# Router rounds, gathers and weight scales of the later experts placed later in TensorE's queue

## The chip, the cores and the metric

One NeuronCore of one Trainium2 chip. The metric is the device time in microseconds (us) of one execution. Engines are named as in the profile: PE is TensorE's matmul side and PEld its weight loads, DVE is VectorE, ACT is ScalarE, POOL is GpSimd, SP is SyncE.

## What is computed

Three layers in a row: an attention with 32 memory slots, an expert layer whose router fills eight experts of 576 tokens each, and a dense gated layer.

```python
# attention, per batch (8) and head (8), sequence 576, head size 64, 32 slots
a = softmax(phi over the sequence);  k_m = a^T k;  v_m = a^T v
x = softmax(q k_m^T / 8) v_m                      # x: 4608 tokens x 512
# expert layer: 8 experts, capacity 4608 / 8 = 576 tokens
logits = x @ w_gate
for idx in argsort(-logits.flatten()):            # best (token, expert) pairs first
    tok, e = idx // 8, idx % 8
    if assigned[tok] >= 0 or counts[e] >= cap: continue
    assigned[tok] = e; counts[e] += 1
out[mask_e] = relu(x[mask_e] @ w1[e]) @ w2[e]     # 512 -> 1024 -> 512
# dense layer, all tokens
h = out @ w_in;  out = (h * clip(h + 3, 0, 6) / 6) @ w_out     # 512 -> 2048 -> 512
```

## The kernel before

The first part, up to about 250 us, is the attention (a software pipeline over 36 steps); it writes x to DRAM (`xd`) and keeps the router's logits in SBUF (`LG`). The second part does the experts two at a time. For each pair P of experts (2P and 2P+1) TensorE runs, in this order: `l1(2P)` (x times w1, tiles `p<-xt,w` of 128x288), `l2(2P)` (times w2, tiles `p<-h,w`), `l1(2P+1)`, `l2(2P+1)`, and `l34(P)`, the dense layer on the pair's 1152 tokens. `l34` is 48 steps; each step is 12 matmuls `p<-yt,wi` of 128x384 (times w_in) and, two steps behind, 9 matmuls `acc<-wo,h` of 128x512 (times w_out). All operands are split in a high and a low fp16 half, so that each product takes three matmuls. Between the two halves of a step ACT, DVE, ACT and POOL turn `p` into the two fp16 halves of `h`.

Experts are found one after the other. `route(k)` finds the expert that fills up next. In up to eight rounds it counts, for 15 thresholds at a time, how many free tokens prefer each expert above the threshold (nine matmuls `rtp<-Bo,C` on the comparison tile `C`, L794; four that add them up, L803; one that spreads the result to all partitions, L812). Then it counts once more (`ce`, L854), numbers the chosen tokens by a prefix sum (`tot`, L881 and L882), and turns the numbers into a list of token indices `ix` by 36 matmuls with one-hot tiles `OH` (L951, in six groups of six; each OH tile is a DVE instruction of 128x768, three buffers). The last expert's route has no rounds. `gathers` then fetches the tokens' rows of `xd` by five indirect DMAs on POOL's queue (`xg<-xd,ix`, two buffers from the third expert on, so that the next fetch follows a transposition), transposes them on TensorE (`xp<-ident,xg`, L623) and lets ACT and DVE write the two halves of `xt`. `weights` fetches the expert's w1 and w2 (`wst`, indirect DMAs on POOL's queue), finds their scale (squares on ACT, `ws` and `s_...m` on DVE, a maximum over the partitions by a TensorE transposition `amx`, L694) and splits them on ACT and DVE (`w<-wst,s`). `ysplit` does the same for the experts' outputs (`sy_...`). Routes 0 and 1 run before the first pair; routes 2P+2 and 2P+3 run inside `l34(P)`, from its step 16 on (`R_OK`).

All this is one instruction stream per engine, and the place of each instruction in it is set when the kernel is built. A clock (`CK.now`) adds up an estimated cost of every dense matmul in `mm`. The router, the gathers, the weights and the evictions are Python generators. After every dense matmul `run` resumes each generator whose time has come; a generator writes its instructions to the streams there and yields the clock time at which it wants to go on, mostly `V_.t + HOP`, the estimated end of DVE's work plus 0.25. So a small matmul that waits for DVE is put into TensorE's stream behind the dense matmuls that the clock thinks will cover DVE's work. TensorE executes its stream in that order.

```python
    def mm(o, l, r, start, stop, cost):
        nc.tensor.matmul(o, l, r, start=start, stop=stop)
        CK.now += cost
        run()
```

The places that the change touches: `all_max` (L688) and `pow2` (L700) for the scales, `route` (L737; its yields at L792, L852, L879 and L942), `weights` (the call of `pow2` at L1009), `gathers` (`fetch`, the time at which a gather counts as landed, L1075) and `ysplit` (L1353).

Of the kernel before, what the change touches and what calls it, by code (L numbers as in the profile page):

```python
# [20 lines left out]
def attn_moe_kernel(ctx: ExitStack, tc: tile.TileContext, q, k, v, phi, w_gate, w1, w2, w_in, w_out, out):  # L21
# [68 lines left out]
    with tc.tile_pool(name="ald", bufs=2) as ald, tc.tile_pool(name="aw", bufs=2) as aw, \  # L90
# [354 lines left out]
        for t in range(-LEAD - 4 - PRE, NTK + A1 + 2):  # L445
# [72 lines left out]
            if t in DT:  # L518
                tag, m = DT[t]
# [60 lines left out]
    V_ = Eng(nc.vector, 0.1, 0.00105)  # L580
    A_ = Eng(nc.scalar, 0.06, 0.00097)
    G_ = Eng(nc.gpsimd, 0.1, 0.0022)
    HOP = 0.25
    DQ = [0.0]

    def dma(cost, issue=None):
        DQ[0] = max(DQ[0], (CK.now if issue is None else issue) + 1.8) + cost
        return DQ[0] + 0.3
# [96 lines left out]
    half_c = rt.tile([128, 1], F32, name="half_c")  # L685
    nc.vector.memset(half_c, 0.5)

    def all_max(m, f):  # L688
        yield V_.t + HOP
        done = [False]  # L690
        while len(MMQ) >= 4 and not MMQ[0][0]:
            yield CK.now + 0.05
        p = mm_tile([128, 128], "amx", done)
        nc.tensor.matmul(p, m.bitcast(F32).to_broadcast([128, 128]), ident, start=True, stop=True)  # L694
        CK.now += 0.22
        yield CK.now + HOP
        V_.tensor_reduce(f, p, axis=AX.X, op=OP.max)
        done[0] = True

    def pow2(src, name, sq, lo, target):  # L700
        m = rt.tile([128, 1], I32, name=name + "m", tag="scm_", bufs=4)
        f = rt.tile([128, 1], F32, name=name + "f", tag="scf_", bufs=4)
        o = rt.tile([128, 2], F32, name=name)
        oi = o.bitcast(I32)
        if sq:
            V_.tensor_scalar(m, src.bitcast(I32), 24, 23, op0=OP.logical_shift_right, op1=OP.logical_shift_left)
            t = target + 127 + 63
        else:
            V_.tensor_scalar(m, src.bitcast(I32), 0x7F800000, None, op0=OP.bitwise_and)
            V_.tensor_scalar(m, m, float(lo << 23), None, op0=OP.max)  # L710
            t = target + 127 + 127
        yield from all_max(m, f)
        SR[0] = SR[0] or sq
        f = f.bitcast(I32)
        V_.tensor_scalar(oi[:, 0:1], f, -1.0, float(t << 23), op0=OP.mult, op1=OP.add)
        V_.tensor_scalar(oi[:, 1:2], f, float((254 - t) << 23), None, op0=OP.add)
        yield V_.t + HOP
        return o
# [16 lines left out]
            yield from route(k)  # L735

    def route(k):  # L737
        V = rt.tile([128, NT], F32, name="V")
        B1 = rt.tile([128, NT, E], F32, name="B1", tag="BC")
        bm = rt.tile([128, NT], F32, name="bm")  # L740
# [20 lines left out]
        else:  # L761
            TH = TH0
            for i in range(NST):
                C = rt.tile([128, NT, 15], BF16, name="C")
                p = ps.tile([128, 64], F32, name="rtp")
                if k == 0:
                    due = []
                    for c0, c1 in ((0, 34), (34, NT)) if i == 0 else ((0, 18), (18, NT)):
                        if i == 0:
                            best(c0, c1)  # L770
                        cmp(C, TH, c0, c1)
                        due.append((c0, c1, V_.t))
                    if i > 1:
                        post()
                    if EM and i:
                        dense_abs(V_, ND[0])
                        BUSY.remove(EM.pop(0))
                        ND[0] += 1
                        early()
                    x_tiles(3 if i else 4)  # L780
                    for c0, c1, v in due:
                        yield v + HOP
                        for t in range(c0, c1):
                            nc.tensor.matmul(p[:15, :E], C[:, t], Bo[:, t], start=(t == 0), stop=(t == NT - 1))
                        CK.now += 0.0243 * (c1 - c0)
                    V_.t = max(V_.t, CK.now + HOP)
                    p1 = p
                else:
                    cmp(C, TH, 0, NT)
                    if i > 1:  # L790
                        post()
                    yield V_.t + HOP  # L792
                    for t in range(9):
                        nc.tensor.matmul(p[:60, :32], C[:, 4 * t:4 * t + 4].rearrange("p t n -> p (t n)"),  # L794
                                         Bo[:, 4 * t:4 * t + 4].rearrange("p t e -> p (t e)"),
                                         start=(t == 0), stop=(t == 8))
                    CK.now += 0.3
                    yield CK.now + HOP
                    V_.tensor_copy(CS[:60], p[:60, :32])
                    yield V_.t + HOP  # L800
                    p1 = ps.tile([128, 64], F32, name="rtp")
                    for t in range(4):
                        nc.tensor.matmul(p1[:15, :E], idh[:60, 15 * t:15 * t + 15], CS[:60, E * t:E * t + E],  # L803
                                         start=(t == 0), stop=(t == 3))
                    CK.now += 0.11
                    yield CK.now + HOP
# [42 lines left out]
        ce = rt.tile([128, E], BF16, name="ce")  # L849
        with nc.allow_low_precision(reason="integers up to 36"):  # L850
            V_.tensor_reduce(ce, BC, axis=AX.X, op=OP.add)
        yield V_.t + HOP  # L852
        p = ps.tile([128, 64], F32, name="rtp")
        nc.tensor.matmul(p[:, :E], onesb, ce, start=True, stop=True)  # L854
        CK.now += 0.03
# [20 lines left out]
        V_.tensor_copy(tot, sc[:, :, NT - 1])  # L876
        if k == 0:
            x_tiles(4)
        yield V_.t + HOP  # L879
        p = ps.tile([128, 64], F32, name="rtp")  # L880
        nc.tensor.matmul(p[:, 0:2], tri, tot, start=True, stop=False)  # L881
        nc.tensor.matmul(p[:, 1:2], triu, tot[:, 0:1], start=False, stop=True)  # L882
# [29 lines left out]
        lo = rt.tile([128, NT], I32, name="lo")  # L912
# [26 lines left out]
            OHP[0] = True  # L939
            x_tiles(7)  # L940
        for q4 in range(6):
            yield (G_ if k == 0 and q4 == 5 else V_).t + HOP  # L942
            if k == 0 and q4 == 4:
                OH.append(ohp)
            elif q4 < 5:
                OH.append(oh(q4 + 1))
            elif k:
                update()
            for t in range(6):
                tt = 6 * q4 + t  # L950
                nc.tensor.matmul(p[:, 0:10], OH[q4][:, t], RH[:, tt].rearrange("p a h -> p (a h)"),  # L951
                                 start=(tt == 0), stop=(tt == NT - 1))
            CK.now += 0.17
            if k == 0:
                x_tiles(2 * NT if q4 == 2 else 2)
# [27 lines left out]
    def weights():  # L983
        for T in range(2 * E):
# [21 lines left out]
                yield CK.now + 0.1  # L1006
            V_.tensor_reduce(s4, sq, axis=AX.X, op=OP.add)
            yield V_.t + HOP
            s = yield from pow2(s4, f"s{which}_{k}", True, 0, (4, 13)[which])  # L1009
            (S1, S2)[which][k] = s  # L1010
            while k and (L1D, L2D)[which].get(k - 1, 0) < (8, 4)[which]:
                yield CK.now + 0.3
# [42 lines left out]
    def gathers():  # L1055
        for k in range(E):
# [7 lines left out]
            def fetch(i):  # L1064
                n = 64 if i == 4 and k % 2 == 0 else 128
                if k == 0:
                    xg = hbuf(3 + i)[:, 0:512]
                elif k == 1 and i > 1:
                    if i % 2 == 0:
                        big.append(wk.tile([128, 2, 512], F32, name="xg", tag=f"wst{i // 2 - 1}"))  # L1070
                    xg = big[-1][:, i % 2]
                else:
                    xg = wk.tile([128, 512], F32, name="xg", tag=f"xg{i % 2}")
                G_.indirect_dma_start(out=xg[:n], out_offset=None, in_=xd, in_offset=U(ap=ix[:n, i:i + 1], axis=0))
                rdy.append(dma(0.75, G_.t))  # L1075
                xgs.append((i, n, xg))
            depth = 2 if k > 1 else 5
            big = []
# [268 lines left out]
    def ysplit(k):  # L1347
# [2 lines left out]
        yield V_.t + HOP  # L1350
        a = absmax(YM[k], f"ymx{k}")
        yield V_.t + HOP
        sy = yield from pow2(a, f"sy_{k}", False, 15, 2)  # L1353
        SY[k] = sy
        P = k // 2
        if k % 2 == 0:
# [177 lines left out]
```

## Time and profile before

| what | value |
|---|---|
| runs of the kernel before | 1522.28, 1526.74, 1525.70 us; median 1525.7 us |
| the profiled execution's own time | 1519.59 us |
| its span, first to last instruction | 1517.7 us |
| PE busy | 1402.9 us, 92% of the span |
| DVE busy | 838.6 us, 55% |
| ACT busy | 734.0 us, 48% |
| POOL busy | 481.0 us, 32% |
| mean granted TensorE clock | 0.975 |

A window's idle time of PE is its length less PE's busy time. The list of waits names for each group of instructions the engine's idle time just before them and what ended it. In the timeline, a row is a run of like instructions on one engine with start, length and count; in brackets stands the idle time before it and what ended that. Ends of matmuls are modelled: the next matmul starts before the end that is shown for the one before.

### The profile page before, as it was taken

How to read it: one execution, taken by the hardware profiler on the slowest of the kernel's cores; microseconds unless marked ns; L12 is line 12 of the kernel's file. 1: busy time of each engine (PE TensorE's matmuls, PEld its weight loads, DVE VectorE, ACT ScalarE, POOL GpSimd, SP SyncE). 2: the span in 40 equal slices, each digit the busy share in tenths (PEclk: the TensorE clock that was granted, in tenths of full speed). 3: DMA queues.
4: the chain of work that ended last, by engine and by line, in shares of the span. 5: the costliest groups of instructions: out<-in, count | busy, mean ns of one | idle time of the engine just before them, and what ended most of it. 6: DMA issues, size and time to landing. Idle time of an engine off the chain costs nothing.

```text
span 1517.7 us, 26287 instructions
## 1 busy us (share of the span) xinstructions
PE 1402.9 (92%) x10506; PEld 931.7 (61%) x10506; DVE 838.6 (55%) x1985; ACT 734.0 (48%) x1419; POOL 481.0 (32%) x557
## 2 busy tenths in 40 slices
PE   4778886898889999999999999999999999999997
PEld 3667765786444445897544458885545588855553
DVE  5788967899985973453158743522477335221111
ACT  3667655577763553453335533623346536233332
POOL 4555305134552533200224332102235311023232
PEclk9989996999999999999999999999999999999999
DMA  9865577355300420200003220200023102000000
GB/s 301 291 229 194 178 254 242 131 179 167 112 27 22 136 78 21 82 17 1 1 22 93 72 70 30 70 1 1 21 67 111 56 29 70 1 0 22 1 21 21
DMA packets 65913, 130.67 MB, mean 86 GB/s; under 512 B 5248, under 2 KB 35968, under 8 KB 65792
## 3 DMA queue, kind: packets, MB, share of 16 engines
q1 hardware_dynamic: 49808, 74.48, 14.9%
q0 software_dynamic: 15168, 52.96, 10.8%
q8 instruction: 82, 1.34, 0.4%
q10 hardware_dynamic: 816, 1.57, 0.3%
q14 instruction: 39, 0.32, 0.1%
HBM read 110.12 MB, written 18.87 MB: 85 GB/s over the span
## 4 chain that ended last, share of the span: by engine, by line
PE 64%; DVE 16%; issue 6%; ACT 6%; DMA 5%; POOL 3%; SPq 0%; ACTq 0%; POOLq 0%; DVEq 0%
PE p L618 37%; PE acc L618 19%; DVE cva L567 4%; PE xa L420 2%; DMA xg<-xd,ix 2%; DMA wst<-in_moe_w_dram,ei 2%; POOL h L567 1%; DVE h L567 1%; PE kvp L191 1%; PE rtp L794 1%; DMA kvt<-in_v_dram 1%; DVE OH L567 1%; ACT wscr L567 1%; ACT h L567 1%; DVE pm L138 1%
## 5 line engine op out<-in xcount | busy, mean ns | idle before, releaser
L618 PE MATMUL p<-yt,wi 128*128 128x384 f16 x2304 | 422.8, 327 | 0.0
L618 PE MATMUL acc<-wo,h 128*128 128x512 f16 x1728 | 418.0, 380 | 4.5 <-ACT h L567 4.0
L567 POOL TENSOR_TENSOR h<-h,h 128x384 f16<-128x384 f32 x192 | 183.7, 957 | 623.6 <-ACT h L567 449.6
L618 PEld LDWEIGHTS <-w 128*128 128x128 f16 x3072 | 339.6, 121 | 49.9 <-issue 4.3
L618 PEld LDWEIGHTS <-wi 128*128 128x128 f16 x2304 | 218.6, 98 | 155.7 <-issue 1.6
L567 DVE SCALAR_TENSOR_TENSOR h<-h,p 128x384 f32<-128x384 f32 x192 | 105.9, 551 | 332.6 <-ACT h L567 317.1
L567 ACT ACTIVATE h<-p,half_c,inv 128x384 f32<-128x384 f32 (+1 forms) x256 | 143.9, 587 | 301.2 <-PE p L618 293.3
L618 PEld LDWEIGHTS <-h 128*128 128x128 f16 x1728 | 163.7, 98 | 173.7 <-ACT h L567 5.6
L618 PE MATMUL p<-xt,w 128*128 128x288 f16 x1536 | 198.0, 288 | 3.7 <-DVE h L567 3.5
L618 PE MATMUL p<-h,w 128*128 128x288 f16 x1536 | 197.3, 288 | 4.3 <-DVE w L567 3.7
L567 ACT ACTIVATE h<-h 128x384 f16<-128x384 f32 x192 | 100.1, 521 | 117.8 <-DVE h L567 116.5
L567 POOL DMA_INDIRECT wst<-in_moe_w_dram,ei x64 | 66.2, 1035 | 110.2 <-DVE tot L567 33.8
L567 DVE SCALAR_TENSOR_TENSOR h<-p,h 128x288 f16<-128x288 f32 x128 | 57.3, 454 | 78.9 <-ACT h L567 78.9
L567 ACT ACTIVATE h<-p 128x288 f16<-128x288 f32 x128 | 52.1, 414 | 90.7 <-PE p L618 89.7
L567 DVE SCALAR_TENSOR_TENSOR w<-wst,s,w 128x512 f16<-128x512 f32 x124 | 94.5, 781 | 2.4 <-ACT w L567 2.4
L567 ACT ACTIVATE w<-wst,s 128x512 f16<-128x512 f32 x124 | 83.7, 715 | 8.5 <-DVE s L567 5.8
L567 DVE SCALAR_TENSOR_TENSOR cva<-dst,cva 128x512 int32<-128x512 int32 (+1 forms) x96 | 82.6, 881 | 0.4 <-ACT dst L567 0.2
L567 DVE TENSOR_REDUCE ym<-y 128x1 f32<-128x288 f32 x64 | 28.8, 450 | 93.8 <-ACT y L567 91.9
L567 ACT ACTIVATE wscr<-wst 128x1024 bf16<-128x1024 f32 x64 | 67.3, 1052 | 19.0 <-DMA wst<-in_moe_w_dram,ei 18.0
L567 ACT ACTIVATE y<-p 128x288 f32<-128x288 f32 x64 | 26.0, 406 | 96.3 <-PE p L618 92.8
L567 POOL DMA_INDIRECT xg<-xd,ix x35 | 36.4, 1040 | 75.1 <-PE xp L623 55.6
L191 PE MATMUL kvp<-kvt,A 128*64 128x128 f32 x576 | 44.6, 309 | 7.3 <-ACT A L170 3.0
(313 smaller groups left out, 1568.5 us busy)
## 6 DMA issues: line engine op xcount, KB each, us to landing
dst<-in_moe_w_out_dram SPq DMA_DIRECT2D x26, 512.0 KB, 3.6
qt<-in_q_dram SPq DMA_DIRECT2D x8, 1024.0 KB, 13.3
dq<-in_moe_w_in_dram SPq DMA_DIRECT2D x16, 512.0 KB, 4.9
xd<-xs SPq DMA_DIRECT2D x32, 256.0 KB, 5.1
kvt<-in_k_dram SPq DMA_DIRECT2D x7, 1152.0 KB, 5.4
kvt<-in_v_dram SPq DMA_DIRECT2D x7, 1152.0 KB, 12.4
dst<-in_moe_w_in_dram SPq DMA_DIRECT2D x15, 512.0 KB, 4.6
ph<-in_phi_dram SPq DMA_DIRECT2D x8, 576.0 KB, 11.0
```

The lines of the kernel that those rows point to most:

```text
L138: nc.vector.tensor_reduce(pm, PH[b].rearrange("p h (r m) -> p h m r", m=M), axis=AX.X, op=OP.max)
L191: nc.tensor.matmul(p[i * 64:(i + 1) * 64, g, 0:128], A[:, hp, r, :], KV[b][:, :, hp, r * 64:(r + 1) * 64], start=(r == 0), stop=(r == R - 1))
L420: nc.tensor.matmul(p[r, g], AT[u][:, half, g, r], VB[b][:, g], start=True, stop=True)
L567: r = f(*a, **kw)
L618: nc.tensor.matmul(o, l, r, start=start, stop=stop)
L794: nc.tensor.matmul(p[:60, :32], C[:, 4 * t:4 * t + 4].rearrange("p t n -> p (t n)"), Bo[:, 4 * t:4 * t + 4].rearrange("p t e -> p (t e)"), ...
```

## The change

For experts from the third on (k of 2 and more) the generators ask for a later clock time: 0.8 us more before each round's first count (L794), 1.6 us more before the counts at L854 and L881 and before each of the six groups of one-hot matmuls (L951), 2.2 us more until a gathered tile counts as landed, 1.5 us more before the transposition of a weight scale, and 3.0 us more before that of the output scale of experts 3, 5 and 7. No instruction is added or removed, and no wait between instructions is; all of them stand in another order.

```diff
-    def all_max(m, f):
-        yield V_.t + HOP
+    def all_max(m, f, late=0.0):
+        yield V_.t + HOP + late
...
-    def pow2(src, name, sq, lo, target):
+    def pow2(src, name, sq, lo, target, late=0.0):
...
-        yield from all_max(m, f)
+        yield from all_max(m, f, late)
...
     def route(k):
+        LATE = 0.0 if k < 2 else 1.6
...
                     cmp(C, TH, 0, NT)
                     if i > 1:
                         post()
-                    yield V_.t + HOP
+                    yield V_.t + HOP + LATE / 2
...
             V_.tensor_reduce(ce, BC, axis=AX.X, op=OP.add)
-        yield V_.t + HOP
+        yield V_.t + HOP + LATE
...
-        yield V_.t + HOP
+        yield V_.t + HOP + LATE
         p = ps.tile([128, 64], F32, name="rtp")
         nc.tensor.matmul(p[:, 0:2], tri, tot, start=True, stop=False)
...
         for q4 in range(6):
-            yield (G_ if k == 0 and q4 == 5 else V_).t + HOP
+            yield (G_ if k == 0 and q4 == 5 else V_).t + HOP + LATE
...
-            s = yield from pow2(s4, f"s{which}_{k}", True, 0, (4, 13)[which])
+            s = yield from pow2(s4, f"s{which}_{k}", True, 0, (4, 13)[which], 1.5 if k > 1 else 0.0)
...
-                rdy.append(dma(0.75, G_.t))
+                rdy.append(dma(0.75, G_.t) + (2.2 if k > 1 else 0.0))
...
-        sy = yield from pow2(a, f"sy_{k}", False, 15, 2)
+        sy = yield from pow2(a, f"sy_{k}", False, 15, 2, 3.0 * (k % 2 and k > 1))
```

Up to the route of the third expert the streams are the same. Lines behind L737 carry a number that is higher by one in the changed kernel (L951 is L952 there).

TensorE's stream, third expert's route, from the prefix sum (`tri`, `triu`) to the first one-hot group. The numbers behind `wi` and `wo` are chunks of the dense weights. Before:

```order
L882 LDWEIGHTS triu_2721
L882 MATMUL rtp_6522<-tot_6511,triu_2721 128x1
L618 LDWEIGHTS wi_9_5286
L618 MATMUL p3_6504<-yt_4688,wi_9_5286 128x384
...
L618 LDWEIGHTS h_5_6421
L618 MATMUL acc0_6125<-wo_7_5446,h_5_6421 128x512
...
L618 LDWEIGHTS wi_10_5363
L618 MATMUL p3_6567<-yt_4688,wi_10_5363 128x384
...
L951 LDWEIGHTS OH_6558
L951 MATMUL rtp_6548<-RH_6546,OH_6558 128x10
```

In the changed kernel:

```order
L883 LDWEIGHTS triu_2721
L883 MATMUL rtp_6575<-tot_6548,triu_2721 128x1
L618 LDWEIGHTS wi_11_5482
L618 MATMUL p3_6571<-yt_4688,wi_11_5482 128x384
...
L618 LDWEIGHTS h_1_6506
L618 MATMUL acc0_6111<-wo_9_5620,h_1_6506 128x512
...
L618 LDWEIGHTS wi_12_5566
L618 MATMUL p3_6627<-yt_4688,wi_12_5566 128x384
...
L952 LDWEIGHTS OH_6610
L952 MATMUL rtp_6601<-RH_6599,OH_6610 128x10
```

The lines of dots stand for like pairs of rows. Between the prefix sum and the first one-hot group stood 5 matmuls of `p`, 9 of `acc` and 3 of `p`; now 10 of `p`, 9 of `acc` and 8 of `p`, which is 10 dense matmuls of 384 columns more. The prefix sum itself stands two chunks of w_in later.

DVE's stream at the same place, from the operand `RH` of the one-hot matmuls on (`h` are evictions of the dense layer). Before:

```order
L567 TENSOR_TENSOR RH<-R_6544,idt 128x360
L567 TENSOR_TENSOR OH<-lo,i_2717 128x768
L567 SCALAR_TENSOR_TENSOR h_6552<-h_6552,p_6504 128x384
L567 TENSOR_TENSOR OH<-lo,i_2717 128x768 x3
L567 SCALAR_TENSOR_TENSOR h_6606<-h_6606,p_6567 128x384
L567 TENSOR_TENSOR OH<-lo,i_2717 128x768 x2
L567 TENSOR_REDUCE ws_6644<-wsq 128x1
```

In the changed kernel:

```order
L567 TENSOR_TENSOR RH<-R_6597,idt 128x360
L567 TENSOR_TENSOR OH<-lo,i_2717 128x768
L567 SCALAR_TENSOR_TENSOR h_6613<-h_6613,p_6571 128x384
L567 TENSOR_TENSOR OH<-lo,i_2717 128x768
L567 SCALAR_TENSOR_TENSOR h_6657<-h_6657,p_6627 128x384
L567 TENSOR_TENSOR OH<-lo,i_2717 128x768
L567 TENSOR_REDUCE ws_6678<-wsq 128x1
L567 TENSOR_SCALAR s_2m<-ws_6678 128x1
L567 TENSOR_TENSOR OH<-lo,i_2717 128x768
L567 SCALAR_TENSOR_TENSOR h_6702<-h_6702,p_6679 128x384
L567 TENSOR_REDUCE s_2f<-amx 128x1
```

The one-hot tiles were up to three in a row; now there is one between two evictions, and the weight scale (`ws`, `s_2m`, `s_2f`) stands among them.

POOL's stream around the gather of the fourth expert, in `l2` of the third: the last stores of the pair before, the fetches of tokens and those of the next weights. Before:

```order
L567 DMA out_dram<-y_7825,ix_4466 4608x512
L567 DMA xg<-xd,ix_7541 128x512 x2
L567 DMA wst_8092<-in_moe_w_dram,ei_7354 128x1024
L567 DMA xg<-xd,ix_7541 128x512
L567 DMA wst_8131<-in_moe_w_dram,ei_7354 128x1024
L567 DMA wst_8167<-in_moe_w_dram,ei_7354 128x1024
```

In the changed kernel:

```order
L567 DMA out_dram<-y_7821,ix_4466 4608x512
L567 DMA xg<-xd,ix_7813 128x512 x2
L567 DMA wst_8090<-in_moe_w_dram,ei_7542 128x1024
L567 DMA wst_8120<-in_moe_w_dram,ei_7542 128x1024
L567 DMA wst_8137<-in_moe_w_dram,ei_7542 128x1024
L567 DMA xg<-xd,ix_7813 128x512
```

The fifth fetch of tokens stood behind one fetch of weights; now it stands behind three.

## Rows read from the trace of the kernel before

**Rows 1.** The page: busy time of the engines.

```profile
PE 1402.9 (92%) x10506; PEld 931.7 (61%) x10506; DVE 838.6 (55%) x1985; ACT 734.0 (48%) x1419; POOL 481.0 (32%) x557
```

**Rows 2.** Windows: stretch and length, busy us of each engine, clock, DMA.

```profile
455.00:604.00 149.00, 143.02 (x982) 73.79 (x981) 93.54 (x254) 68.42 (x127) 56.08 (x59) 1.00 0.20 65
...
767.00:917.00 150.00, 145.13 (x994) 75.02 (x993) 93.86 (x254) 69.71 (x129) 56.37 (x60) 1.00 0.20 65
...
1080.00:1221.00 141.00, 135.54 (x872) 71.23 (x870) 79.44 (x193) 68.46 (x127) 54.62 (x60) 1.00 0.22 69
```

**Rows 3.** Waits of PE, 455 to 1260 us: us in total, times, longest.

```profile
PE rtp L951 <- DVE OH L567: 7.9, 5, 1.7
PE xp L623 <- DMA xg<-xd,ix: 4.5, 6, 1.4
PE rtp L794 <- DVE C L567: 2.0, 3, 1.1
PE rtp L881 <- DVE tot L567: 1.3, 1, 1.3
PE rtp L854 <- DVE ce L567: 0.9, 1, 0.9
PE xp L623 <- DVE w L567: 0.8, 1, 0.8
```

**Rows 4.** Timeline of PE: a scale of expert 1, one-hot groups that waited, a dense stretch.

```profile
390.17 0.46 PE L694 MATMUL amx<-ident,sy_1m 128*128 128x128 f32 x2 [4.42 <-DVE sy_1m L567]
...
502.19 0.30 PE L951 MATMUL rtp<-RH,OH 128*128 128x10 bf16 x6 [1.49 <-DVE OH L567]
...
567.21 0.31 PE L951 MATMUL rtp<-RH,OH 128*128 128x10 bf16 x6 [1.75 <-DVE OH L567]
...
889.32 2.11 PE L618 MATMUL p<-yt,wi 128*128 128x384 f16 x12
891.27 2.10 PE L618 MATMUL acc<-wo,h 128*128 128x512 f16 x9
893.21 2.11 PE L618 MATMUL p<-yt,wi 128*128 128x384 f16 x12
```

**Rows 5.** The tiles sl and OH on DVE, 455 to 1260 us: ns min/median/max.

```profile
L567 DVE TENSOR_TENSOR sl<-scn x6: 195/923/1658, 498.1 to 1147.1; 128x36 f32<-128x36 f32 x6
L567 DVE TENSOR_TENSOR OH<-lo,i x36: 944/948/1674, 501.2 to 1160.3; 128x768 bf16<-128x768 int32 x36
```

**Rows 6.** Timeline of DVE, third expert's route: its numbering, then the next route's start.

```profile
498.13 1.66 DVE L567 TENSOR_TENSOR sl<-scn 128x36 f32<-128x36 f32 x1
...
512.60 1.56 DVE L567 TENSOR_TENSOR Bo<-B,bm 128x288 bf16<-128x288 f32 x1
...
515.62 0.75 DVE L567 SCALAR_TENSOR_TENSOR w<-wst,s,w 128x512 f16<-128x512 f32 x1
```

**Rows 7.** Timeline of POOL: beside that numbering, and in the fourth expert's gather.

```profile
498.80 0.93 POOL L567 TENSOR_TENSOR h<-h,h 128x384 f16<-128x384 f32 x1
...
633.92 1.45 POOL L567 DMA_INDIRECT xg<-xd,ix  x1 [0.30 <-DVE xt L567]
...
640.96 0.94 POOL L567 DMA_INDIRECT wst<-in_moe_w_dram,ei  x1 [0.81 <-DVE w L567]
```

**Rows 8.** Timeline of PE: the third expert's first count.

```profile
456.69 0.44 PE L794 MATMUL rtp<-Bo,C 128*60 128x32 bf16 x9 [1.14 <-DVE C L567]
```

**Rows 9.** Timeline of PE: l1 of the third expert; gather and l1 of the fourth.

```profile
604.24 1.63 PE L618 MATMUL p<-xt,w 128*128 128x288 f16 x12
...
637.90 0.63 PE L623 MATMUL xp<-ident,xg 128*128 128x128 f32 x4 [0.49 <-DMA xg<-xd,ix]
...
642.64 0.63 PE L623 MATMUL xp<-ident,xg 128*128 128x128 f32 x4 [0.81 <-DVE w L567]
643.11 10.70 PE L618 MATMUL p<-h,w 128*128 128x288 f16 x86
...
659.25 1.02 PE L618 MATMUL p<-xt,w 128*128 128x288 f16 x7
```

## The prediction

> **What bounds the kernel now.** I read the page first, then PE's windows, PE's list of waits, and the timelines around those waits. TensorE is busy for 1402.9 us, far ahead of DVE's 838.6 [rows 1], and from 455 us on its clock stands at 1.00 of the higher level, 2.4 GHz, in the windows read [rows 2]. So from there the time is the dense matmuls plus what TensorE waits between them. The three stretches in which routes run beside the dense layer have idle time of 149.00 - 143.02 = 5.98, 150.00 - 145.13 = 4.87 and 141.00 - 135.54 = 5.46 us [rows 2]. The list of waits from 455 us on has six lines: 7.9, 4.5, 2.0, 1.3, 0.9 and 0.8, together 17.4 us in 17 waits [rows 3]. The reader should see that each line is a small matmul of a route or a gather. No dense matmul and no scale (`amx`) is among them. TensorE executes its stream in order, so every such wait holds up dense work that stands ready behind it. That is what the change can reach: 17.4 us. The wait of 4.42 us for the output scale of expert 1 [rows 4] is not reached, since the 3.0 us apply to experts 3, 5 and 7 alone; nor is anything ahead of the third expert's route.
>
> **The change part by part.** Nothing is added, so the only cost can be a wait that something placed later makes elsewhere. A dense matmul of 384 columns costs (891.27 - 889.32) / 12 = 0.163 us, one of `acc` (893.21 - 891.27) / 9 = 0.216 us [rows 4].
>
> *One-hot groups, 7.9 us in five waits* (routes of the third to the seventh expert) [rows 3]. In each route the first group waits, 1.49 us in the third expert's and 1.75 us in the fourth's [rows 4]. In the third expert's stream 10 more matmuls of 384 columns stand ahead of it: 10 x 0.163 = 1.63 us, more than 1.49. In the fourth's I count 7 of these and 2 of `acc` more: 1.14 + 0.43 = 1.57 us, which leaves 1.75 - 1.57 = 0.18. The pattern repeats in the other pairs, so 0.18 us is left twice. Gain 7.9 - 0.4 = 7.5. The later groups follow each other at intervals of at least 2.5 us of dense work, against 0.95 us for a one-hot tile [rows 5], so they need nothing.
>
> *Gathers, 4.5 + 0.8 us in seven waits* [rows 3]. 2.2 us more until a tile counts as landed is more than the longest, 1.4. Gain 5.3. The place to watch is POOL's queue in `l2` of the third expert: the fifth fetch now stands behind the third fetch of weights, which started at 640.96 and took 0.94, as it waits for the splits on DVE [rows 7]. From 641.9 the landing takes what the fourth fetch took, 637.90 - 633.92 = 3.98 us [rows 7, 9], so to 645.9. Its transposition stood at 642.64, or 641.34 without the two waits of 0.49 and 0.81 [rows 9]. By the stream, 39 more matmuls of 288 columns now stand between the first and the fifth transposition, and two more ahead of the first: 41 x 10.70 / 86 = 5.1 us [rows 9]. That makes 646.4, 0.5 us behind the landing. I take no wait; the bounds are 0 and 1 us in each of three such gathers.
>
> *First counts of routes, 2.0 us in three waits* [rows 3]. The third expert's waits 1.14 us [rows 8], and one `acc` and four 384-column matmuls more stand ahead: 0.216 + 0.65 = 0.87. Left 0.27, gain 0.9. The two others are of the fourth and sixth expert, (2.0 - 1.14) / 2 = 0.43 each. There the last one-hot group is followed by 7.1 us of matmuls instead of 5.1, but on DVE the updates of the logits and one more split `w` of 0.75 us [rows 6] now stand in that interval, where they stood outside it. Bounds for each: gone, or 1.2 us instead of 0.43. I take no gain.
>
> *Counts `ce` and `tot`, 0.9 + 1.3 us* [rows 3], each below the 1.6 us that is added. Gain 2.2.
>
> *Scales.* Without an `amx` among the waits [rows 3] there is nothing to gain. The delay is covered: the third expert's split began at 515.62 us [rows 6] and its l1 at 604.24 [rows 9], so some 12 us more are hidden by the dense layer. The output scale of expert 3 is due at step 16 of the next dense layer, 16 x 3.89 = 62 us behind its start. Cost nothing; if that cover were gone, 1.5 to 3 us a piece.
>
> The sum: 7.5 + 5.3 + 0.9 + 2.2 = 15.9, so 16 us. The profiled execution took 1519.6 us and would take 1503.6. The median of the runs shown is 6.1 us above it; against that, 1525.7 - 16 = 1509.7. I forecast **1510 us**. What a measurement of this kernel can tell from no change is about 0.3%, 4.6 us.
>
> **What speaks against it: POOL beside DVE.** `sl` took between 195 and 1658 ns and a one-hot tile between 944 and 1674 ns for the same work [rows 5]. In the third expert's chain `sl` ran from 498.13 to 499.79 while POOL made a low half `h`, 498.80 to 499.73 [rows 6, 7]. One such stretch of 1.658 - 0.195 = 1.46 us lies in that chain already and is in the wait. The new stream shifts the chain against POOL's work. With a second one in each of the five chains 5 x 1.46 = 7.3 us would come back. The Trainium skill (SBUF — State Buffer, section Who interferes with whom) says that a DVE instruction with two SBUF inputs contends with a GpSimd instruction that reads SBUF, and that the loser is blocked for the other's whole instruction. By that rule such stretches stay as likely wherever the chain stands, and the pair of rows above agrees with it.
>
> **The rivals.**
>
> *Part of the waits comes back* (24%). All of the above: 7.3 us by second stretches in the one-hot chains, 3 x 1 us in the fifth fetches behind weights, 2 x 0.8 us in the first counts of the fourth and sixth expert (`Bo` was stretched to 1.56 us there [rows 6]). At worst 11.9 us come back and 4 are left: 1521.7; at half, 10 us are left: 1516. For it: DVE is busy 63% in these stretches, 93.54 of 149 us [rows 2], and the estimates that place the matmuls know nothing of stretches. Against: a second stretch needs POOL twice within one chain of 4 us, and POOL makes one `h` in a step of 3.9 us.
>
> *No change* (8%), 1525 us. The change would not do what it says if DVE's instructions moved back as far as the matmuls that wait for them, for the one-hot tiles are written at the times of the groups. For it: there were three tiles in a row, now there is one between two evictions. Against: the first tile, on which the waits of 1.49 and 1.75 us ended, still follows its operand directly on DVE.
>
> *Slower* (4%). The gathers of the fourth, sixth and eighth expert must end before their l1. The fifth transposition of the fourth's starts at 642.64 and l1 at 659.25 [rows 9]: 16.6 us, and 659.25 - 646.4 - 1.3 (the waits that are gone) = 11.6 us by the new stream. The eviction of the tile takes some 1.5 us of that. If the weights' fetches held the fifth fetch 10 us longer than I worked out, TensorE would stop before l1. To use up the 16 us and be 5 us slower, it takes 21 / 3 = 7 us more in each of the three, so 17 us of delay each: 1531 us. Against it: the third fetch of weights began 7 us behind the fourth fetch of tokens [rows 7], and nothing in the change makes the splits slower.
>
> **How the numbers follow.** Forecast as worked out, 64%; part comes back, 24%; no change, 8%; slower, 4%. The range begins below 1510 by what the run-to-run difference between the median and the profiled execution allows, 6 us, and by the 2 us that the waits' short ends may hide (17 waits of about 0.1 us), and ends at the worst of the second case: 1502 to 1522. It leaves out the last two cases. Faster by over 0.3% (below 1521.1): 64% and 22 of the 24: 86%. Within 0.3%: 2 + 8 = 10%. Slower: 4%.
>
> **What would show it.** PE's waits from 455 us on fall from 17.4 to 2 us or less; the one-hot line falls to below 0.5 us; the gather's lines are gone; the wait of 4.42 us for expert 1 is still there. The three route stretches last some 5 us less each, and the stretches without routes are the same. I am wrong if the lines of `OH`, `C` or `xg` keep more than half their time, if a dense matmul appears in the list (`p<-xt,w` for want of `xt`, `acc` for want of `h`), or if the idle time goes and the span does not.

## The result, and the profile after

The changed kernel takes 1504.31 us in the median of 6 runs (1503.2 to 1509.55), the kernel before 1526.22 us beside it (6 runs, 1521.42 to 1528.29): a ratio of 0.9882, 95% interval 0.9862 to 0.9902, 15 to 21 us less (the two medians themselves lie 21.9 us apart). The profiled execution took 1503.65 us where before it took 1519.59: 15.9 us less, with a span of 1501.6 us.

The page's line of busy times, after:

```profile
PE 1397.4 (93%) x10506; PEld 931.4 (62%) x10506; DVE 835.3 (56%) x1985; ACT 732.6 (49%) x1419; POOL 487.8 (32%) x555
```

The windows after (columns as in [rows 2]: stretch and length, busy us of PE, PEld, DVE, ACT and POOL, clock, DMA):

```profile
455.00:604.00 149.00, 147.86 (x1013) 78.17 (x1012) 91.60 (x248) 68.96 (x129) 55.74 (x58) 1.00 0.19 62
...
767.00:917.00 150.00, 149.38 (x1033) 81.79 (x1031) 92.00 (x248) 69.67 (x131) 58.89 (x63) 1.00 0.21 66
...
1080.00:1221.00 141.00, 138.32 (x900) 79.50 (x898) 75.99 (x181) 67.77 (x128) 55.45 (x57) 1.00 0.21 69
```

The idle time in these windows fell from 5.98, 4.87 and 5.46 us [rows 2] to 1.14, 0.62 and 2.68. They are the same times and not the same work, for the changed kernel is further on by then. Measured by the work, from the third expert's first count or the first `p<-yt,wi` of a dense layer to the next `p<-xt,w`, the three stretches with routes last 141.4, 204.4 and 199.1 us, where they lasted 147.6, 210.1 and 202.9; the stretches without routes changed by 0.6 us or less. The list of PE's waits from 455 to 1260 us (total us, times, longest), against 17.4 us in 17 waits before [rows 3]:

```profile
PE xp L623 <- DMA xg<-xd,ix: 2.1, 4, 1.0
PE rtp L855 <- DVE ce L567: 1.7, 1, 1.7
PE rtp L795 <- DVE C L567: 1.2, 3, 0.5
PE acc L618 <- DVE y L567: 0.4, 1, 0.4
```

The one-hot line is gone; 5.4 us in 9 waits are left. PE's timeline shows the wait for expert 1's scale, which the change does not reach (4.42 us in [rows 4]), the third expert's first count (1.14 us in [rows 8]), its first one-hot group (1.49 us in [rows 4]), the fifth fetches of the fourth and eighth expert, and the wait for the eighth expert's `ce`, which was the 0.9 us of [rows 3] and is now longer:

```profile
390.09 0.77 PE L694 MATMUL amx<-ident,sy_1m 128*128 128x128 f32 x2 [5.45 <-DVE sy_1m L567]
...
456.72 0.44 PE L795 MATMUL rtp<-Bo,C 128*60 128x32 bf16 x9 [0.28 <-DVE C L567]
...
507.96 0.30 PE L952 MATMUL rtp<-RH,OH 128*128 128x10 bf16 x6
...
640.88 0.63 PE L623 MATMUL xp<-ident,xg 128*128 128x128 f32 x4 [0.31 <-DMA xg<-xd,ix]
...
1145.59 0.18 PE L855 MATMUL rtp<-ce,onesb 128*128 128x8 bf16 x1 [1.72 <-DVE ce L567]
...
1247.53 0.63 PE L623 MATMUL xp<-ident,xg 128*128 128x128 f32 x4 [1.00 <-DMA xg<-xd,ix]
```

**Where the 15.9 us are.** Up to the third expert's first count the two streams are the same, and that count starts at 456.69 and at 456.72 us. From it to the last `acc` matmul it was 1052.4 us and is 1036.5: all of the gain. By the distances between matmuls' starts, the listed waits account for 13.3 us of it (idle time 17.5 - 5.5 = 12.0, and for each of the 8 waits less some 0.16 us more: a matmul's modelled end lies that far behind the start of the next, so a wait is longer than the idle time listed for it), shorter gaps that the list leaves out for 2.9 (17 of them before, 4 after), and the rest of the stream for -0.3. This stretch, written "first count to end", is the measure used below. What lies ahead of it varies from run to run: over the profiles of this study the third expert's first count starts between 454.6 and 467.3 us, though the stream ahead of it is the same in all kernels but the last.

### The profile page after: what moved, and what is told of

It is laid out like the page before. It is cut to its first block, busy times and chain, and to the rows that moved or that the text cites. A ratio compares the mean times of both kernels' runs of the same rounds, so it can differ in the third digit from the quotient of the medians.

```text
span 1501.6 us, 26275 instructions
## 1 busy us (share of the span) xinstructions
PE 1397.4 (93%) x10506; PEld 931.4 (62%) x10506; DVE 835.3 (56%) x1985; ACT 732.6 (49%) x1419; POOL 487.8 (32%) x555
## 4 chain that ended last, share of the span: by engine, by line
PE 67%; DVE 14%; ACT 5%; issue 5%; DMA 4%; POOL 2%; SPq 0%; ACTq 0%; POOLq 0%; DVEq 0%
PE p L618 39%; PE acc L618 21%; DVE cva L567 4%; DMA xg<-xd,ix 2%; PE xa L420 1%; DMA ph<-in_phi_dram 1%; PE kvp L191 1%; DMA wst<-in_moe_w_dram,ei 1%; DVE w L567 1%; ACT h L567 1%; PE rtp L795 1%; DVE pm L138 1%; PE xp L623 1%; DVE h L567 1%; POOL h L567 1%
## 5 line engine op out<-in xcount | busy, mean ns | idle before, releaser
L618 PE MATMUL p<-yt,wi 128*128 128x384 f16 x2304 | 417.6, 327 | 0.0
L567 POOL TENSOR_TENSOR h<-h,h 128x384 f16<-128x384 f32 x192 | 187.3, 976 | 634.5 <-ACT h L567 492.6
L567 ACT ACTIVATE wscr<-wst 128x1024 bf16<-128x1024 f32 x64 | 67.3, 1052 | 13.3 <-DMA wst<-in_moe_w_dram,ei 12.6
```

The costliest lines, as they stand in the source:

```text
L567: r = f(*a, **kw)
```

## The experiments

Two theories are set against each other. **Own waits**: each wait belongs to its matmul, so each part of the change gains its own term of the prediction, alone or with the others, and the scales gain nothing. **Handed over**: DVE, ACT and the fetches as a whole run behind the clock that the builder adds up; a wait anywhere lets them catch up, and where one is taken away, the next small matmul with too little cover (dense work ahead of it in the stream) waits in its place. The first runs named a third, **spreading**: it gains to set small matmuls apart, whichever they are. The four parts, as they are set back from the changed kernel:

```diff
 one-hot groups
-            yield (G_ if k == 0 and q4 == 5 else V_).t + HOP + LATE
+            yield (G_ if k == 0 and q4 == 5 else V_).t + HOP
 gathers
-                rdy.append(dma(0.75, G_.t) + (2.2 if k > 1 else 0.0))
+                rdy.append(dma(0.75, G_.t) + 0.0)
 counts (first counts; in the same way ce and tot)
-                    yield V_.t + HOP + LATE / 2
+                    yield V_.t + HOP
 scales (in the same way the output scale)
-            s = yield from pow2(s4, f"s{which}_{k}", True, 0, (4, 13)[which], 1.5 if k > 1 else 0.0)
+            s = yield from pow2(s4, f"s{which}_{k}", True, 0, (4, 13)[which])
```

### One part alone

Three parts set back, one kept.

Only the one-hot groups: 

> Only the 1.6 us more ahead of the six one-hot groups are kept; counts, gathers and scales ask for the times of the kernel before. If the time falls by what TensorE waits less: the line of OH in TensorE's waits from 455 us on goes from 7.9 us to below 0.5, those of xg, C, ce, tot stay within 1 us each of 4.5, 2.0, 0.9, 1.3, and the span falls by 8 to 9 us (7.9 and some 0.15 for each of five waits, as much as the modelled ends cover). If the gain of the change is not from these waits but from the small matmuls being spread in general, it falls by about a quarter of 16, 4 us. If one part alone gains nothing since the next wait takes it over, by less than 2 us.

Only the gathers: 

> Only the 2.2 us more until a gathered tile counts as landed are kept. If the time falls by what TensorE waits less: the two lines of xp (4.5 and 0.8 us) go to some 1.5 us together, what is left being the fifth fetch behind the fetches of weights in l2 of the third, fifth and seventh expert; the lines of OH, C, ce, tot stay as before, and the span falls by 4 to 5 us. If the gain is from spreading in general, some 4 us with the OH line changed too. If the next wait takes it over, less than 2 us.

Only the counts: 

> Only the counts are kept later: 0.8 us ahead of each round's first count, 1.6 us ahead of ce and tot. If the time falls by what TensorE waits less: C goes from 2.0 to about 1.1 (the fourth and sixth expert's keep theirs), ce and tot from 2.2 to between 0 and 1.7, the rest stays, and the span falls by 1.5 to 3.5 us. If the gain is from spreading in general, this part moves the most matmuls (40 rounds) and falls most, by 6 us or more.

Only the scales: 

> Only the 1.5 us for weight scales and the 3.0 us for output scales are kept. No amx stands among TensorE's waits from 455 us on, so by the waits there is nothing to gain: the six lines stay within 0.5 us of 7.9, 4.5, 2.0, 1.3, 0.9, 0.8 and the span within 1.5 us of before. If spreading in general is what gains, 2 to 4 us less. If the delay of the scales costs something, a line of p<-xt,w or p<-h,w waiting for w appears.

| kept | ratio to before (95%) | first count to end, us | against before, 1052.4 | PE's listed waits in it, us (before 17.5) | clock falls |
|---|---|---|---|---|---|
| one-hot groups | 1.0025 (1.0005 to 1.0045) | 1058.6 | +6.2 | 18.2 | 4 |
| gathers | 0.9976 (0.9959 to 0.9993) | 1052.0 | -0.4 | 17.2 | 0 |
| counts | 0.9987 (0.9966 to 1.0007) | 1054.0 | +1.6 | 17.0 | 2 |
| scales | 1.0037 (1.0018 to 1.0056) | 1057.3 | +4.9 | 19.4 | 2 |

A clock fall is a stretch at the lower clock, shown below. The stretch comes from one profile of each kernel, the ratio from 12 executions; for the gathers and the counts the ratio is a little better than the stretch (1 to 6 us less, and 5 less to 1 more).

Added up, the four make the stretch 12.3 us longer; together they make it 15.9 us shorter. So own waits fails: the one-hot groups alone should have gained 7.5 us and cost 6.2. Spreading fails too, for it had the one-hot groups gain 4 us and the counts 6 or more. No theory had a part make the kernel slower, but for a word on the scales, and there by waits for `w` that did not appear. The column of waits says what happened: whichever part is kept, some 17 to 19 us of waits are there as before, on other lines, and what the kernels lose is mostly the clock falls. PE's waits with only the one-hot groups late, 455 to 1260 us:

```profile
PE xp L623 <- DMA xg<-xd,ix: 4.9, 6, 1.4
PE rtp L795 <- DVE C L567: 4.3, 3, 2.0
PE amx L694 <- DVE s_2m L567: 2.8, 1, 2.8
PE rtp L855 <- DVE ce L567: 2.5, 1, 2.5
PE amx L694 <- DVE s_6m L567: 1.2, 1, 1.2
```

The 7.9 us of the one-hot line are gone, as its own term said. But the first counts went from 2.0 [rows 3] to 4.3, `ce` from 0.9 to 2.5, and weight scales, of which no line stood before, wait 2.8, 1.2 and less. The largest, in the third expert's route, on PE, DVE and ACT:

```profile
508.79 0.79 PE L694 MATMUL amx<-ident,s_2m 128*128 128x128 f32 x2 [2.79 <-DVE s_2m L567]
```

```profile
504.73 0.95 DVE L567 TENSOR_TENSOR OH<-lo,i 128x768 bf16<-128x768 int32 x1
508.39 0.16 DVE L567 TENSOR_REDUCE ws<-wsq 128x1 f32<-128x4 f32 x1 [2.71 <-ACT wscr L567]
508.58 0.15 DVE L567 TENSOR_SCALAR s_2m<-ws 128x1 int32<-128x1 int32 x1
```

```profile
507.21 1.06 ACT L567 ACTIVATE wscr<-wst 128x1024 bf16<-128x1024 f32 x1 [1.34 <-DMA wst<-in_moe_w_dram,ei]
```

The weight scale now stands among the one-hot tiles in DVE's stream. Its last square on ACT waits for the weights' fetch, `ws` on DVE waits for ACT, and the maximum on TensorE for both: a chain that no line of the list before showed. That DVE, ACT and the fetches run behind the builder's clock as a whole is the reading offered here; the two times were not set side by side.

**The clock fell too.** After that wait TensorE ran at the lower of its two levels, 1.2 GHz. Three windows of that kernel (columns as above), ahead of the end of the wait, at the lower clock and behind it:

```profile
505.30:508.70 3.40, 0.70 (x4) 0.10 (x1) 0.66 (x3) 2.06 (x7) 0.91 (x1) 1.00 0.02 7
508.70:512.10 3.40, 3.31 (x15) 1.71 (x16) 2.85 (x7) 2.72 (x6) 1.45 (x1) 0.50 0.00 0
512.10:515.50 3.40, 3.40 (x26) 1.86 (x25) 2.93 (x5) 2.12 (x5) 1.22 (x1) 1.00 0.08 10
```

15 matmuls ran in the second window and 26 in the third. At a clock of 0.50 half of the 3.4 us is lost, so by this estimate some 1.7 us, on top of the wait. The kernels before and after have no such fall between the first count and the last `acc` matmul. With each fall at half its length, and the waits and gaps as above, the stretch of every kernel of this study comes out to within 1.5 us, that of the kernel with all times doubled (below) to within 4.5.

### One part left out

One part set back, three kept.

Without the scales: 

> The change without the 1.5 us for weight scales and the 3.0 us for output scales. Theory own waits (each part removes the waits of its own line and nothing else): as the change, span within 1.5 us of 1501.6, since the kernel before had no waits at amx. Theory hand-over (DVE runs behind the build's clock, and the wait lands on the first small matmul that has too little dense work ahead of it): waits at amx for the weight scales come up as they did with the one-hot groups alone, 5 to 6 us in five waits, and the part of the time from the first dense layer on is 4 to 7 us longer than in the change.

Without the gathers: 

> The change without the 2.2 us until a gathered tile counts as landed. Own waits: the lines of xp come back to 5.3 us from 2.1, some 3 us longer than the change. Hand-over: the landing of a fetch is DMA's and not DVE's lateness, so it is not handed on by DVE; but a transposition that stands earlier lets the instructions of DVE behind it start earlier in its stream too: 3 to 8 us longer, with waits at C or at OH beside those at xp.

Without the counts: 

> The change without the 0.8 us ahead of first counts and the 1.6 us ahead of ce and tot. Own waits: C, ce and tot come back to 4.2 us from 2.9, some 1.5 us longer than the change. Hand-over: with the one-hot groups alone C had 4.3 and ce 2.5 us, and these come back or more: 5 to 9 us longer than the change.

Without the one-hot groups: 

> The change without the 1.6 us ahead of the one-hot groups. Own waits: the line of OH comes back at 7.9 us, 8 to 9 us longer than the change. Hand-over: the counts alone left 9.0 us at OH, so 8 to 10 us at OH and 9 to 12 us longer than the change; by this part alone the two theories hardly differ.

| left out | ratio to before (95%) | first count to end, us | against after, 1036.5 | PE's listed waits in it, us (after 5.5) | clock falls |
|---|---|---|---|---|---|
| scales | 0.9955 (0.9931 to 0.9980) | 1045.2 | +8.7 | 11.4 | 2 |
| gathers | 0.9948 (0.9929 to 0.9967) | 1045.9 | +9.4 | 12.3 | 2 |
| counts | 0.9979 (0.9962 to 0.9997) | 1049.1 | +12.6 | 13.1 | 3 |
| one-hot groups | 0.9979 (0.9957 to 1.0002) | 1048.7 | +12.2 | 13.7 | 2 |

Each part is worth more when the others are there than its own term said: 8.7 us instead of nothing for the scales, 9.4 instead of 5.3, 12.6 instead of 0.9 + 2.2, 12.2 instead of 7.5. Some 6 to 8 us of each are waits and 3.4 to 5.1 clock falls. Handed over had said 4 to 7, 3 to 8, 5 to 9 and 9 to 12, each less than was measured, so that theory has the direction and not the size. The waits gather where the cover was left out. PE's list, without the gathers, without the counts and without the one-hot groups, one fence each:

```profile
PE xp L623 <- DMA xg<-xd,ix: 12.0, 8, 2.7
PE rtp L795 <- DVE C L567: 0.3, 1, 0.3
```

```profile
PE rtp L795 <- DVE C L567: 8.9, 5, 2.7
PE rtp L855 <- DVE ce L567: 2.9, 1, 2.9
```

```profile
PE rtp L952 <- DVE OH L567: 7.2, 4, 3.4
PE rtp L952 <- DVE s_3m L567: 2.1, 1, 2.1
```

The gathers waited 5.3 us before [rows 3], when other waits gave the fetches time, and 12.0 once those were gone; the first counts 2.0 and then 8.9. Without the scales the list has three `amx` of 0.9 us each, where 5 to 6 us in five waits were expected, 4.6 us of first counts and 1.9 of `ce`: a little wait at a scale, and the rest one step further on. That is handed over. Without the gathers it is seen less well: the waits at `C` or `OH` that were expected beside those of the gathers are 0.3 us.

### Half and double

```diff
-        LATE = 0.0 if k < 2 else 1.6
+        LATE = 0.0 if k < 2 else 0.8
```

and so for the gathers (1.1) and scales (0.75 and 1.5); doubled in the same way (3.2; 4.4; 3.0 and 6.0).

Half: 

> All added times halved (0.4 for first counts, 0.8 for ce, tot and one-hot groups, 1.1 for gathers, 0.75 and 1.5 for scales). If each wait is its own, each keeps what the half does not cover: about 4.0 of the 7.9 us of the one-hot groups (5 x 0.8), 0.5 of the 5.3 of the gathers, 1.4 of the 2.0 of the first counts, 0.6 of the 2.2 of ce and tot, 6.5 us in all; from the third expert's first count to the last acc matmul 1036.5 + 5 = 1042 us, total some 9 to 10 us below the kernel before. If waits are handed over, less than a third of the gain: 1047 us or more in that stretch, total within 5 us of the kernel before, 10 us of waits or more from 455 us on, and the clock at half after some of them.

Double: 

> All added times doubled. Both theories see the same limit: the routes of the fourth and sixth expert end so late that in the order the third to fifth transposition of the odd expert's gather stand in a row, 1.3 us ahead of l1, in pairs 2 and 3. The fifth fetch can only follow the third transposition (two buffers), lands about 4 us later and has to be evicted (1.5 us): l1 starts some 5 us late, twice, with a clock fall of 1.7 us each: +10 to +14 us against the change, less at most 4 us of waits that are left there. 1043 to 1050 us from the first count to the end, total 3 to 12 us below the kernel before. If the limit does not decide, it is as fast as the change or faster (1036 us or less).

Half gave 1048.6 us in the stretch, ratio 0.9976 (0.9958 to 0.9995): 3.8 us of the 15.9. That is the number of handed over, though no clock fall came with it. PE's waits, 455 to 1260 us:

```profile
PE xp L623 <- DMA xg<-xd,ix: 5.0, 7, 1.6
PE rtp L882 <- DVE tot L567: 4.2, 6, 1.3
PE rtp L952 <- DVE OH L567: 3.6, 6, 0.9
```

The one-hot line keeps 3.6 us (own waits said 4.0), but `tot` rose from 1.3 to 4.2 and the gathers stay at 5.0. The gain does not come in proportion; it comes when all of the chain is covered.

Double gave 1054.3 us, ratio 0.9993 (0.9971 to 1.0015): all of the gain lost. The place was right and the size was not: it was expected to be 4 to 11 us better, and one of the two waits had not been seen. The three stretches with routes went on shrinking, by 3.3, 2.3 and 2.6 us against the change. But the stretches of `l1` and `l2` between them, for the second and the third pair of experts, became 13.5 and 13.8 us longer (115.1 and 115.2 us). PE's waits, its timeline ahead of the fourth expert's `l1`, the fifth fetch on POOL, and one window:

```profile
PE xp L623 <- ACT yt L567: 6.4, 2, 3.2
PE amx L694 <- DVE sy_2m L567: 4.3, 1, 4.3
PE amx L694 <- DVE sy_4m L567: 4.3, 1, 4.3
```

```profile
658.22 0.79 PE L694 MATMUL amx<-ident,sy_2m 128*128 128x128 f32 x2 [4.28 <-DVE sy_2m L567]
658.80 1.91 PE L623 MATMUL xp<-ident,xg 128*128 128x128 f32 x8
663.90 1.09 PE L623 MATMUL xp<-ident,xg 128*128 128x128 f32 x4 [3.18 <-ACT yt L567]
```

```profile
660.14 1.30 POOL L567 DMA_INDIRECT xg<-xd,ix  x1 [5.39 <-DVE sy L567]
```

```profile
658.00:668.00 10.00, 6.60 (x28) 5.24 (x29) 8.38 (x19) 6.47 (x15) 1.30 (x1) 0.50 0.10 26
```

Three transpositions stand in a row ahead of `l1`, as the order showed. What was not seen: nothing dense is left there, so the output scale of the third expert stands ahead of them, where in the changed kernel it stands 4 us inside `l1`, and TensorE waits for it as well (4.28 us). The second wait (3.18 us) is put down to ACT's `yt` by the list, but the fifth fetch, which can only follow the third transposition, was issued at 660.14, and its last signal of landing came at 663.77, 0.13 us before the fifth transposition began: that wait is the fetch's as well, as expected. Together 7.5 us of waits, and 10 us at a clock of 0.50.

### A late gather, and one more wait aimed at

```diff
-                rdy.append(dma(0.75, G_.t) + (2.2 if k > 1 else 0.0))
+                rdy.append(dma(0.75, G_.t) + (10.0 if k > 1 else 0.0))
```

> The change with 10.0 us instead of 2.2 until a gathered tile counts as landed, the rest as in the change. In the order the fifth transposition of the odd experts' gathers then stands 0.5 us of dense work ahead of l1, in all three pairs; it is the rival of a late gather. The two halves of xt take about 1.5 us to write, so l1 waits about 1 us in each pair: +3 us if waits are their own (1040 us from the first count to the end), total some 13 us below the kernel before. If each such wait brings a clock fall of 1.7 us and hands itself on to the splits and evictions behind it, +8 us or more (1044.5 us or more). If nothing happens at l1, the point from which the rival decides lies later still.

Measured: 1047.0 us, +10.5 against the change, ratio 0.9950 (0.9928 to 0.9973). That is the size of the second case, and the prediction's rival of the late gather: the stretches of `l1` and `l2` of the second, third and fourth pair last 5.7, 2.9 and 3.7 us longer, with a clock fall in the first and the last. PE's waits show, as in the kernel with all doubled, that it is the output scale of the expert before that is caught ahead of `l1` (in the last pair too, where the wait of 2.97 us is listed under ACT's `w`):

```profile
PE amx L694 <- DVE sy_4m L567: 3.1, 1, 3.1
PE amx L694 <- DVE sy_2m L567: 3.1, 1, 3.1
```

Two of the waits, with a window from the fall of the clock on for the first and one of the same length behind the other:

```profile
662.92 0.79 PE L694 MATMUL amx<-ident,sy_2m 128*128 128x128 f32 x2 [3.10 <-DVE sy_2m L567]
...
974.14 0.49 PE L694 MATMUL amx<-ident,sy_4m 128*128 128x128 f32 x2 [3.11 <-DVE sy_4m L567]
```

```profile
662.30:669.10 6.80, 6.18 (x26) 4.46 (x27) 4.99 (x13) 3.09 (x6) 0.00 (x0) 0.50 0.00 0
974.10:980.90 6.80, 6.76 (x55) 6.76 (x56) 6.22 (x14) 4.53 (x11) 0.00 (x0) 1.00 0.00 1
```

The waits are alike, and only the first has a fall of the clock: 26 matmuls ran in its window, and 55 in the other.

The last experiment adds to the change what it left out:

```diff
-        sy = yield from pow2(a, f"sy_{k}", False, 15, 2, 3.0 * (k % 2 and k > 1))
+        sy = yield from pow2(a, f"sy_{k}", False, 15, 2, 3.0 * (k % 2 and k > 1) + 6.0 * (k == 1))
```

> The change and 6.0 us more ahead of the maximum for the output scale of expert 1, which TensorE waited 5.45 us for at 390 us, at half clock afterwards. If the wait is its own, it goes with the clock fall: 5.5 + 1.7 = 7 us, total about 1497 us where the change has 1504, ratio to the kernel before about 0.984. If waits are handed over: DVE's evictions of the dense layer stand behind the same conversions (cva) that delay sy_1m, so the wait turns into waits for h of 2 us or more at 390 to 400 us, and at most 4 us are gained (1500 us or more).

Measured: 1507.66 us, ratio 0.9897 (0.9868 to 0.9926): the same as the change. The wait of 5.45 us for `sy_1m` is gone, and this stands in its place on PE; below it three windows, ahead of that wait, up to it and behind it:

```profile
394.66 3.59 PE L618 MATMUL acc<-wo,h 128*128 128x512 f16 x9 [3.87 <-ACT h L567]
```

```profile
384.00:389.00 5.00, 5.00 (x34) 3.15 (x33) 5.00 (x8) 3.10 (x7) 2.01 (x2) 1.00 0.58 200
389.00:394.60 5.60, 1.79 (x12) 0.88 (x9) 5.46 (x16) 4.30 (x8) 2.39 (x2) 0.97 0.33 101
394.70:398.00 3.30, 3.30 (x9) 1.22 (x10) 3.30 (x6) 2.68 (x5) 2.25 (x2) 0.55 0.50 159
```

DVE is busy 5.00 of 5.00 and 5.46 of 5.60 us: the conversions `cva` of the dense weights take most of it, and the evictions `h` stand behind them as `sy_1m` did. PE's waits from 376 us to the third expert's first count were 5.5 + 4.3 us and a few tenths and are 7.8 + 1.4; that first count comes 77.1 us after the start of the dense layer instead of 76.6. One wait handed over, seen by itself. From the first count on the stream is that of the change, and the stretch is 1036.4 us beside 1036.5; the last dense layer, in which no route runs, lasts 186.8 us in all 14 profiles. So the stretch repeated to 0.1 us the one time it was taken twice, and all but one of the differences in the tables are far above that (the -0.4 of the gathers alone is nearly nothing). Whether a clock fall comes at the same place in every execution is not shown, for each kernel was profiled once.

## Why the prediction was right, and where its steps were not

The forecast was 1510 us, the median is 1504.3, inside 1502 to 1522; the profiled execution was forecast at 1503.6 and took 1503.65. The sum of 15.9 us is that between the two profiled executions. The 5.7 us from the forecast to the median come from another term: 6.1 us were added for the distance of the median from the profiled execution, and in the changed kernel that distance is 0.7. The sum is right as a whole and not in all its parts; the listed waits, which it is made of, fell by 12.0 us and not by 15.9, and the experiments show that its terms are not to be had one by one.

- *One-hot groups*, 7.5 of 7.9 us: all gone, and the first group of the third expert's route no longer waits. Right, with the others there; alone the part costs 6.2 us.
- *Gathers*, 5.3 us: 2.1 are left, in four waits, so 3.2 are gained. The place named, the fifth fetch behind weights, waits 0.31 us in the fourth expert's gather and 1.00 in the eighth's, within the bounds of 0 and 1; I had taken 0.
- *First counts*, 0.9 of 2.0 us: 1.2 are left, as worked out (1.1); the third expert's kept 0.28 where 0.27 was left, the two others 0.46 and 0.48 where 0.43 each was.
- *`ce` and `tot`*, 2.2 us: 0.5 gained. `tot` is gone; `ce` of the eighth expert waits longer than before, 1.72 us, behind the 1.6 us that were added. DVE's timelines ahead of it, before and after, and POOL's after:

```profile
1138.58 0.24 DVE L567 TENSOR_SCALAR G<-V,th 128x36 f32<-128x36 f32 x1
```

```profile
1141.91 2.43 DVE L567 TENSOR_SCALAR G<-V,th 128x36 f32<-128x36 f32 x1
...
1145.08 0.45 DVE L567 TENSOR_REDUCE ce<-BC 128x8 bf16<-128x288 f32 x1
```

```profile
1141.53 0.94 POOL L567 DMA_INDIRECT wst<-in_moe_w_dram,ei  x1 [0.30 <-DVE Bo L567]
1142.49 1.80 POOL L567 TENSOR_TENSOR h<-h,h 128x384 f16<-128x384 f32 x2
```

  `G`, on 36 elements, took 2.43 us instead of 0.24 and ended 0.05 us after POOL's two `h` (1142.49 + 1.80 = 1144.29). So the rival "part comes back" happened, once on PE's path instead of five times, and in `G` instead of `sl`; the third expert's `sl` still met an `h` and took 1.51 us, now without a wait on PE. The Trainium skill (SBUF — State Buffer, section Who interferes with whom) lists `tensor_scalar` among the DVE operations that can take the ports shared with GpSimd, where whoever issues first keeps them and the other is blocked for that whole instruction. The rows agree that `G` ended with POOL's work and not that the later one is held: `G` began 0.58 us before the first of the two `h`, while POOL issued a fetch. The pair that the prediction called agreeing is the same: `sl` began at 498.13 and `h` at 498.80 [rows 6, 7]. So it is in all six `sl` of 1.5 us and more before and after: they begin during a fetch's issue that an `h` follows within 0.02 us, and end 0.06 or 0.07 us behind that `h`; the six others took 0.20.
- *Scales*, nothing: this is the step that failed. It said that without an `amx` among the waits there was nothing to gain. Left out, they cost 8.7 us. A list of waits shows where TensorE happened to be stopped, not which chains are too tight; waits of 0.5 to 2.8 us at `amx` came up once the one-hot groups no longer waited ahead of them. Alone, the scales' part gains nothing, as the step said, and costs 4.9 us.
- What listed waits were left beyond the forecast (5.4 us, not 1.5) was made up by 0.16 us of each wait gone, 1.3 us, for which the prediction allowed 2 us in the range alone, and by 2.9 us of gaps too short for the list, which it did not have. That the sum came out to the tenth is luck, and so is the profiled execution's 1503.65 us: what lies ahead of the first count varied by 12.7 us over the profiles and happened to be the same in these two.
- *Slower*, a late gather: real, but not at 2.2 us; at 10 us it brings back 10.5 of the 15.9. The place was right; the point of 17 us was too far and the price was not that of the fetch, but of the output scale that is caught ahead of `l1`, and of the clock.
- The signs named held in part. Held: the one-hot line is gone, the route stretches are 6.2, 5.6 and 3.8 us shorter (some 5 forecast), the others are nearly the same, the wait for expert 1 is still there. Did not hold: 5.4 us of waits are left and not 2 or less, and the gathers' line is not gone. Of the signs of being wrong two came in small: the line of `C` kept more than half of its time (1.2 of 2.0 us, which the prediction's own sum already left there), and one dense `acc` waits 0.4 us.

## To carry to other kernels

In a stream whose order is fixed when it is built, a list of waits gave the size of what all small waits together were worth here, but not shares for single lines: a wait that is taken away alone moves to the next hand-over with too little cover. So give all hand-overs of a chain their slack at once, among them those that show no wait, and judge it by the sum. It pays while the producing engines have idle time (DVE at 54 to 63% in the route stretches), not where one is full (DVE at 5.46 of 5.60 us ahead of 395 us), and it ends where the work made later meets the next stage's start.

## What was not expected of the hardware

Short waits in an otherwise dense stream of matmuls could be followed by a stretch at TensorE's lower level, 1.2 GHz, which by the estimate above cost 1.7 us each where it lasted 3.4 us: so after 2.79 us in the kernel with the one-hot groups alone, after 1.77 (531.4 us, a gather) with the counts alone, and after two of 1.16 and 1.05 us, 1.5 us apart (528.8 us, again with the one-hot groups alone). Others were not: 1.72 us for `ce` after the change, 2.46 (840.4 us, a gather) without the gathers' part, and 3.11 with the late gather, where a wait of 3.10 of the same kind in the same kernel was. Which of two like waits is followed by a fall is left open. No run here changed the clock by itself.
